# The last two rows of an attention layer get buffers of their own and are normed on VectorE

## The chip, the cores and the metric

The kernel runs on one core of one Trainium2 chip. A core has five engines that run side by side and meet only at semaphores: TensorE (PE; its weight loads are listed as PEld), VectorE (DVE), ScalarE (ACT), GpSimd (POOL) and SyncE (SP), which here only issues DMA transfers. SBUF is the memory on the chip, in 128 partitions; PSUM is the small memory into which TensorE accumulates; DRAM is outside.

The metric is the device time of one execution in microseconds (us), as the median of several runs. Before the change it is 1166.17 us over 3 runs (1164.17 to 1168.2).

## The reference

The program is four layers on a sequence of S = 2048 positions with D = 576 channels, in the order A, B, A, B. Each layer adds its output to its input, and each takes the layer norm of its input first.

```python
x = x + _A_ref(_layernorm(x), A_wqkv, A_wo)
x = x + _B_ref(_layernorm(x), B_w_in, B_w_sp, B_b_sp, B_w_out)
x = x + _A_ref(_layernorm(x), A_wqkv, A_wo)
x = x + _B_ref(_layernorm(x), B_w_in, B_w_sp, B_b_sp, B_w_out)
```

A is attention with 32 heads of 18 channels. A position attends to itself and to seven earlier ones, two apart (a window of 8, dilation 2); the output goes through `wo`.

B is a gated layer with F = 4608:

```python
z = _gelu(einsum('bsd,df->bsf', x, w_in))
z1 = z[..., :Fh]
z2 = _layernorm(z[..., Fh:])
g = einsum('ts,bsf->btf', w_sp, z2) + b_sp[None, :, None]
return einsum('bsf,fd->bsd', z1 * g, w_out)
```

with Fh = F/2 = 2304. The layer norm is `(x - mean) / sqrt(var + 1e-5)`.

## The kernel before

**Rows.** The 2048 positions are 16 row tiles of 128 (NS = 16), one position per partition. In an A layer, row tile `i` holds even positions for `i` below 8 and odd ones above (`rows_of`), since with dilation 2 these do not see each other. The normed input of every layer stands transposed in SBUF, as `xnT` (channels on partitions, positions along it).

**Layer A** lays out Q and K through staging tiles `stg` (PG, with many small transfers), then runs 34 steps (`NST = 2 * NT`): logits (L473), exp on ScalarE (L482), the product with V (PV, L496 to L504). The work of the tail of the layer is hung on those steps in `table`, with `at(step, function, arguments)`; what is hung on a step is issued after PV of that step, in the order in which it was hung, and what is hung past the last step is issued at the end, in order of step. For row tile `i` the pieces are:

- `WO(i, hh)`: five matmuls into `pw` (L557), and an add on VectorE of `pw` and the old x into half of the new x (L560). `x_new` is a ring of four buffers. So the x of row tile `i` takes the buffer of row tile `i - 4`, and waits until that one's norm has read it and its store has landed.
- `XST(i)`: SyncE stores the new x to DRAM (`xres`).
- `LN_STATS`, `LN_AGGR`, `LN_POW`: statistics of the row (L568), mean and variance (L574) and the addition of eps (L581) on VectorE; the power -1/2 on GpSimd (L582).
- `LN_XN(i)`: the norm itself, on GpSimd (`ln_xn`, L259), and a copy of the last 64 channels (L262), into one of four bf16 buffers.
- `XN_ST(i)`: SyncE stores the normed row to a DRAM tensor, `xn_rows`.
- `LN_T(k)`: SyncE reads 128 natural positions of `xn_rows` back with a transposing DMA (L598) into `xnT`. Tiles `2m` and `2m + 1` each need the even and the odd row tile `m` and `m + 8`.

The last four row tiles (12 to 15, `tail_rows`) end too late for the steps. Their statistics, powers and norms all hang on step 37 (`NST + 3`), in two pairs: statistics of 12 and 13, their powers, their norms, and then the same for 14 and 15. The store of the normed row 15 and the transposes of tiles 14 and 15 are put into `deferred`, from which the next layer issues them when it needs those rows. The order on all five engines is the order of the program here (`manual_schedule`).

**Layer B, first part** (p1): the matmuls of z2 (L907) in nine groups of eight units, a unit being 128 positions by 512 channels in a PSUM bank; rows are taken in pairs, nine units to a pair. ScalarE empties the banks through gelu into a row buffer `zp` (L954; three buffers), VectorE takes statistics (L956, L969), GpSimd takes eps and power (L971, L972), and the norm into `Z` (L980) is split: VectorE does eight ninths, GpSimd the last ninth. A `zp` buffer is free again only when both have read it. VectorE and ScalarE work in the order of the program in p1; on SyncE a scheduler chooses the order. In this part it also loads the spatial weights, four `Wq` tiles of 128 x 16 x 512, with transposing DMAs (L877), the bias `b_sp`, and the first z1 weights, which go into a part of `Z` not used so far.

**Layer B, second and third part**: z1 (L1031), the spatial product (L1055) with its gate (L1059, L1060) and the output product (L1104). SBUF of one layer is used again by the next: `Z` of layer B covers the places of `QK` and of the first staging tiles of layer A. A write to such a place waits for those who used it last.

Of the kernel before, what the change touches and what calls it, by code (L numbers as in the profile page):

```python
# [12 lines left out]
f32 = mybir.dt.float32  # L13
# [5 lines left out]
P = 128  # L19
D = 576  # L20
# [43 lines left out]
class K:  # L64
# [274 lines left out]
    def layer_A(self, li):  # L339
        nc, tc, cfg = self.nc, self.tc, self.cfg  # L340
        S, NT, XW, NS = cfg.S, cfg.NT, cfg.XW, cfg.NS
# [12 lines left out]
        stgs = [main.tile([P, 2, CBW], bf16, name=f"stg{k_}") for k_ in range(NSTG if li == 0 else 2)]  # L354
# [11 lines left out]
        sb = sb_cm.__enter__()  # L366
        x_news = [sb.tile([P, D], f32, name="x_new", tag="x_new", bufs=4) for k_ in range(4)]
# [92 lines left out]
        NST = 2 * NT  # L460
# [27 lines left out]
        def PV(s):  # L488
            t, hf = divmod(s, 2)
            nk, nq = tdim(t)  # L490
            O_ps = self.PT_tile([P, 512], f32, "O_ps")
            for jp, js in enumerate(((0, 1, 2), (3,))):
                for ftl in range(4):
                    for jj, j in enumerate(js):
                        idx = 4 * ftl + j
                        nc.tensor.matmul(O_ps[:, idx * (DH + 1):(idx + 1) * (DH + 1)],  # L496
                                         lhsT=P_bufs[2 * jp + s % 2][:nk, jj, ftl, :],
                                         rhs=v_ext[:nk, t, 16 * hf + idx, :], start=True, stop=True)
            Ov = O_ps[:, 0:16 * (DH + 1)].rearrange("p (h e) -> p h e", e=DH + 1)
            o_t = o_bufs[t % len(o_bufs)]  # L500
            rec = sb.tile([P, 16], f32, name="rec", tag="rec", bufs=2)
            nc.vector.reciprocal(out=rec[:], in_=Ov[:, :, DH])
            LN_AGGR()
            nc.vector.tensor_tensor(out=o_t[:, 288 * hf:288 * (hf + 1)].rearrange("p (h d) -> p h d", d=DH),  # L504
                                    in0=Ov[:, :, 0:DH], in1=rec[:, :, None].to_broadcast([P, 16, DH]), op=ALU.mult)
            LN_POW()
            if hf == 1 and t < NT - 2:
                if in_ring(t):
                    c0 = q0_(t) % (RING * P)
                    n0 = min(P, RING * P - c0)  # L510
                    nc.sync.dma_start_transpose(out=oT[:, :, c0:c0 + n0], in_=o_t[0:n0, :])
                    if n0 < P:
                        nc.sync.dma_start_transpose(out=oT[:, :, 0:P - n0], in_=o_t[n0:P, :])
                else:
                    nc.sync.dma_start_transpose(out=o_slots[(t // 2) % NSLOT][:], in_=o_t[:, :])
# [16 lines left out]
                nc.scalar.copy(out=oT[:, :, c0:c0 + n], in_=pt[:, :, a:a + n])  # L532

        tails = {}
        xnd = self.dram.tile([S, 640], bf16, name=f"xn_rows{li}")

        def xo_of(p):
            if li == 0:
                return p % 3
            return p % 2 if p < 4 else (2, 0, 1)[(p - 4) % 3]  # L540
# [9 lines left out]
        def WO(i, hh):  # L550
            st = tails[i]
            if hh == 0:
                st["x"] = x_news[i] if i < 4 else sb.tile([P, D], f32, name="x_new", tag="x_new", bufs=4)
            r0 = (i % RING) * P
            pw = self.PT_tile([P, 512], f32, "pw")
            for c in range(5):
                nc.tensor.matmul(pw[:, 0:288], lhsT=oT[:, c, r0:r0 + P], rhs=wo_sb[:, c, hh * 288:(hh + 1) * 288],  # L557
                                 start=(c == 0), stop=(c == 4))
            hs = slice(hh * 288, (hh + 1) * 288)
            nc.vector.tensor_tensor(out=st["x"][:, hs], in0=pw[:, 0:288], in1=st["xo"][:, hs], op=ALU.add)  # L560
# [9 lines left out]

        def LN_AGGR():
            for i, st in owed:
                mv = sb.tile([P, 2], f32, name="ln_mv", tag="ln_mv", bufs=3)
                nc.vector.bn_aggr(out=mv[:], in_=st[:])  # L574
                tails[i]["ln"] = mv

        def LN_POW():
            for i, _ in owed:
                mv = tails[i]["ln"]
                rstd = sb.tile([P, 1], f32, name="ln_rstd", tag="ln_rstd", bufs=3)  # L580
                nc.vector.tensor_scalar(out=rstd[:], in0=mv[:, 1:2], scalar1=EPS, scalar2=None, op0=ALU.add)  # L581
                nc.gpsimd.tensor_tensor(out=rstd[:], in0=rstd[:], in1=self.neg_half[:], op=ALU.pow)  # L582
                tails[i]["ln"] = mv, rstd, None
            owed.clear()

        def LN_REST():
            LN_AGGR()
            LN_POW()

        def LN_XN(i):  # L590
            mv, rstd, nmr = tails[i].pop("ln")
            tails[i]["xn"] = self.ln_xn(tails[i]["x"], P, mv, rstd, nmr, eng="pool")

        def XN_ST(i):
            self.dma(self.rows_of(xnd, i), tails.pop(i)["xn"])
# [155 lines left out]
        def at(s, f, *a):  # L751
            table.setdefault(s, []).append((f, a))
# [27 lines left out]
        tail_rows = []  # L780
        for i in range(NS):
            s, s1 = wo_steps[i]
            if i % 2 == 0:
                last = [j for j in range(i) if xo_of(j // 2) == xo_of(i // 2)][-1:]
                at(max([s - 7] + [wo_steps[j][1] + 1 for j in last]), XO, i)
            at(s, WO, i, 0)
            at(s1, WO, i, 1)
            if s1 < NST - 1:
                at(s1, LN_STATS, i)
                at(s1 + 1, LN_XN, i)  # L790
            else:
                tail_rows.append(i)
            at(s1 + 1, XST, i)
            if i < NS - 1:
                at(s1 + 4, XN_ST, i)
            if NS // 2 <= i < NS - 1:
                for k_ in range(2):
                    at(max(s1 + 6, NST + 3 * (i - NS // 2) - 4), LN_T, 2 * i - NS + k_)
        for k_ in range(0, len(tail_rows), 2):
            for i in tail_rows[k_:k_ + 2]:  # L800
                at(NST + 3, LN_STATS, i)
            at(NST + 3, LN_REST)
            for i in tail_rows[k_:k_ + 2]:
                at(NST + 3, LN_XN, i)
        at(2 * (NT - 3) + 3, O_CP, NT - 3)
        if li == 0:
            at(0, self.load_wo, nc.sync)
# [28 lines left out]
        for s in sorted(table):  # L836
            for f, a in table[s]:
                f(*a)
        self.deferred.append(((NS - 2) * P, lambda: XN_ST(NS - 1)))
        for k_ in (NS - 2, NS - 1):  # L840
            self.deferred.append((k_ * P, lambda k_=k_: LN_T(k_)))
        man.__exit__(None, None, None)
# [374 lines left out]
```

## Time and profile before

| | |
|---|---|
| median of 3 runs | 1166.17 us (1164.17 to 1168.2) |
| the profiled execution, its span from the first to the last instruction | 1170.2 us |
| mean granted TensorE clock | 0.997 |
| p1 of the first layer B, from its first matmul to the first of z1 | 126.39 to 201.93 us |
| p1 of the second layer B | 702.62 to 775.80 us |
| POOL `ln_xn` L259, one norm of 128 x 576 | 2.29 us, 32 of them |
| ACT `zp` waiting for POOL `Z`, first and second p1 | 9.2 and 10.8 us in all |
| PE `pzs` waiting for ACT `zp`, first and second p1 | 1.0 and 0.5 us |

The profile is of one execution, recorded by the hardware. Of the profiled execution only the span is known; no other time stands beside it. Its views are: a page with the busy time of each engine; the busy time by stretches, with the granted TensorE clock; the chain of work that ended last, followed back from the end; the instructions of an engine in order of time; and the groups of like instructions. In the rows in order of time, the first number is the start in us from the beginning of the span and the second the time that the merged instructions took; a bracket at the end tells how long the engine was idle before the row, and which instruction released it. SPq rows are DMA issues: the time of a row is the issue, not the transfer. In the chain, a DMA row is a transfer from issue to landing.

### The profile page before, as it was taken

How to read it: one execution, taken by the hardware profiler on the slowest of the kernel's cores; microseconds unless marked ns; L12 is line 12 of the kernel's file. 1: busy time of each engine (PE TensorE's matmuls, PEld its weight loads, DVE VectorE, ACT ScalarE, POOL GpSimd, SP SyncE). 2: the span in 40 equal slices, each digit the busy share in tenths (PEclk: the TensorE clock that was granted, in tenths of full speed). 3: DMA queues.
4: the chain of work that ended last, by engine and by line, in shares of the span. 5: the costliest groups of instructions: out<-in, count | busy, mean ns of one | idle time of the engine just before them, and what ended most of it. 6: DMA issues, size and time to landing. Idle time of an engine off the chain costs nothing.

```text
span 1170.2 us, 19968 instructions
## 1 busy us (share of the span) xinstructions
PE 1150.5 (98%) x8163; PEld 612.5 (52%) x8258; DVE 550.0 (47%) x1167; ACT 338.8 (29%) x493; POOL 278.8 (24%) x389
## 2 busy tenths in 40 slices
PE   9999999999999999999999999999999999999998
PEld 5457544444444444457755774444444444444677
DVE  8668598322333332244555886963322223322321
ACT  5589455111100111101247884541011110111000
POOL 4659865000000000001153786640000000000000
PEclk9999999999999999999999999999999999999999
DMA  9599697000000000049646997930000000001332
GB/s 217 119 160 294 193 212 142 23 12 12 12 1 12 12 12 1 6 138 296 169 107 105 204 256 182 242 91 1 12 12 12 12 12 1 12 1 46 111 105 74
DMA packets 183240, 106.45 MB, mean 91 GB/s; under 512 B 135225, under 2 KB 164441, under 8 KB 183149
## 3 DMA queue, kind: packets, MB, share of 16 engines
q1 hardware_dynamic: 170285, 84.85, 31.6%
q0 software_dynamic: 6512, 14.57, 4.8%
q10 hardware_dynamic: 6352, 5.75, 1.6%
q8 instruction: 64, 1.05, 0.4%
q14 instruction: 27, 0.22, 0.1%
HBM read 42.40 MB, written 21.77 MB: 55 GB/s over the span
## 4 chain that ended last, share of the span: by engine, by line
PE 85%; POOL 7%; DMA 3%; DVE 2%; issue 2%; ACT 0%; SPq 0%; POOLq 0%; DVEq 0%; ACTq 0%
PE pg L1055 42%; PE po L1104 12%; PE pz L1031 6%; PE pz1s L1031 6%; PE pzs L907 5%; PE pp L436 4%; PE pz L907 4%; POOL ln_xn L259 4%; PE pv L410 2%; PE O_ps L496 1%; PE pw L557 1%; PE L_ps L473 1%; POOL ln_rstd L582 1%; DMA QK<-stg 1%; DMA o_slot<-o_t 1%
## 5 line engine op out<-in xcount | busy, mean ns | idle before, releaser
L1055 PE MATMUL pg<-Wq,Z 128*128 128x512 bf16 x2260 | 497.9, 379 | 2.5
L1055 PEld LDWEIGHTS <-Z 128*128 128x128 bf16 x2304 | 225.5, 98 | 271.8
L1059 DVE TENSOR_TENSOR g_tmp<-pg,ln_xn 128x512 f32<-128x512 f32 x144 | 99.6, 692 | 421.5 <-PE pg L1055 419.5
L1050 ACT ACTIVATE z1T<-pz 128x1024 bf16<-128x1024 f32 x36 | 34.9, 1021 | 500.8 <-PE pz L1031 500.8
L78 POOL DMA_DIRECT2D wout<-in_B_w_out_dram x4 | 4.3, 1070 | 598.8 <-PE pg L1055 598.8
L1104 PE MATMUL po<-wout,Z 128*128 128x288 bf16 x1152 | 141.4, 286 | 0.0
L482 ACT ACTIVATE P_sb<-L_ps 128x1440 bf16<-128x1440 f32 (+3 forms) x136 | 125.1, 972 | 21.1 <-PE L_ps L473 19.7
L1104 PEld LDWEIGHTS <-Z 128*128 128x128 bf16 x1152 | 112.7, 98 | 28.8
L907 PEld LDWEIGHTS <-xnT 128*128 128x128 bf16 (+1 forms) x800 | 68.7, 98 | 80.0 <-issue 15.5
L1060 DVE TENSOR_TENSOR Z<-g_tmp,z1T 128x512 bf16<-128x512 f32 x144 | 99.7, 692 | 12.2
L956 DVE BATCH_NORM_STATS2 z_st<-zp 128x6 f32<-128x512 bf16 (+1 forms) x160 | 91.0, 617 | 5.1 <-ACT zp L954 4.8
L1031 PEld LDWEIGHTS <-w 128*128 128x128 bf16 (+1 forms) x640 | 53.7, 97 | 74.0 <-issue 13.6
L436 PE MATMUL pp<-xnT,wqk_sb 128*128 128x512 bf16 x341 | 82.2, 382 | 2.5 <-DVE o_t L504 1.3
L259 POOL TENSOR_SCALAR ln_xn<-x_new,ln_mv,ln_rstd 128x576 bf16<-128x576 f32 x32 | 73.3, 2291 | 2.6
L1114 DVE TENSOR_TENSOR x_new<-po,xo 128x288 f32<-128x288 f32 (+1 forms) x64 | 28.8, 455 | 87.4 <-PE po L1104 83.9
L1031 PE MATMUL pz<-xnT,w 128*128 128x512 bf16 (+1 forms) x316 | 66.3, 380 | 0.2
L1031 PE MATMUL pz1s<-xnT,w 128*128 128x512 bf16 (+1 forms) x310 | 64.9, 379 | 0.9 <-issue 0.8
L78 POOL DMA_DIRECT2D QK<-stg x81 | 49.5, 614 | 46.0 <-DVE oT L524 14.8
L907 PE MATMUL pzs<-win2a,xnT 128*128 128x512 bf16 (+1 forms) x235 | 59.9, 364 | 0.4 <-issue 0.3
L907 PE MATMUL pz<-win2a,xnT 128*128 128x512 bf16 (+1 forms) x233 | 58.3, 357 | 0.6 <-issue 0.2
L980 POOL TENSOR_SCALAR Z<-zp,z_mv,z_rstd 128x256 bf16<-128x256 bf16 x32 | 55.7, 1740 | 3.4
L436 PEld LDWEIGHTS <-wqk_sb 128*128 128x128 bf16 x360 | 33.5, 98 | 38.3 <-DVE o_t L504 1.5
(113 smaller groups left out, 936.6 us busy)
## 6 DMA issues: line engine op xcount, KB each, us to landing
xres<-x_new SPq DMA_DIRECT2D x48, 288.0 KB
xo<-xres SPq DMA_DIRECT2D x32, 288.0 KB
wout<-in_B_w_out_dram POOLq DMA_DIRECT2D x4, 1296.0 KB, 8.2
xn_rows<-ln_xn SPq DMA_DIRECT2D x32, 160.0 KB
w<-in_B_w_in_dram SPq DMA_DIRECT2D x16, 256.0 KB
QK<-stg POOLq DMA_DIRECT2D x55, 72.0 KB, 5.2
xo<-xres SPq DMA_DIRECT2D x6, 576.0 KB
QK<-stg SPq DMA_DIRECT2D x39, 72.0 KB
```

Of the source, the lines that this page charges most:

```text
L78: return eng.dma_start(out=out, in_=in_)
L259: e.tensor_scalar(out=xn[:nrows, 0:D], in0=x_t[:nrows, :], scalar1=mv[:nrows, 0:1], scalar2=rstd[:nrows, 0:1], op0=ALU.subtract, op1=ALU.mult)
L436: nc.tensor.matmul(pp[:, :], lhsT=w, rhs=self.xnT[:, c, cc * 512:(cc + 1) * 512], start=(c == 0), stop=(c == 4))
L482: nc.scalar.activation(out=P_bufs[2 * jp + s % 2][:nk, :, :, 0:nq], in_=Lv[:nk, :, :, 0:nq], func=ACT.Exp, scale=scale)
L907: nc.tensor.matmul(out[:, o0:o0 + n], lhsT=self.xnT[r0:r1, c, r * P:(r + 1) * P], rhs=win2(c)[r0:r1, w0:w0 + n], start=start, stop=stop, t ...
L956: nc.vector.bn_stats(out=st[:, x // 512, :], in_=zp[:, x:x + min(512, w0 + n - x)])
L980: eng.tensor_scalar(out=Z[:, b0:b1, i, :], in0=zv[:, b0:b1, :], scalar1=mv[:, 0:1], scalar2=rstd[:, 0:1], op0=ALU.subtract, op1=ALU.mult)
L1031: nc.tensor.matmul(outs[a_], lhsT=w1[r0:r1, c, sub * P:(sub + 1) * P], rhs=self.xnT[r0:r1, c, q * 512:(q + 1) * 512], start=start, stop=st ...
L1055: nc.tensor.matmul(pg[:, :], lhsT=Z[:, jj, i, sub * P:(sub + 1) * P], rhs=Wq[q][:, i, :], start=(i == 0), stop=(i == NS - 1))
L1059: nc.vector.tensor_tensor(out=tmp[:], in0=pg[:, :], in1=bsp[:, qs], op=ALU.add)
L1060: nc.vector.tensor_tensor(out=uT(jj)[:, sub, qs], in0=tmp[:], in1=z1Ts[jj, sub][:, qs], op=ALU.mult)
L1104: nc.tensor.matmul(acc[hh], lhsT=u_rows(j, i), rhs=wouts[j // NJH][:, j % NJH, hh * 288:(hh + 1) * 288], start=(j == 0), stop=(j == NJ - 1))
```

## The change

In layer A of both kinds (first and second):

- `late_rows` cuts the first two staging tiles `stg` into a float32 part of 576 (a row's x) and a bf16 part of 640 (its normed row). `WO` uses them for row tiles 14 and 15 instead of the `x_new` ring, and `LN_XN` writes their normed rows there.
- `LN_XN` of row tiles 14 and 15 goes to VectorE; 12 and 13 stay on GpSimd.
- All statistics and powers of the four tail rows are issued first, and the four norms after them, so that GpSimd's four powers stand ahead of its two remaining norms. `ln_mv` and `ln_rstd` get five buffers each instead of three.
- The stores of the normed rows 14 and 15 are hung on step 37, the last ones of that step, ahead of those of 12 and 13 (step 38). The transposes of tiles 4 and 5 move from step 36 to step 38, behind the stores of 14 and 15. The store of row 15 is no longer deferred.

In the program that comes out, TensorE and ScalarE have the same instructions in the same order as before. On SyncE the order after row 10's normed store is: x of 12 and 13, normed 11, x of 14 and 15, normed 14 and 15, transposes 4 and 5, normed 12 and 13, ten transposes (6 to 15), the first `Wq`, `b_sp`, three `Wq`, and then the first z1 weights (`Z<-in_B_w_in_dram`), which the scheduler had placed before the normed stores of 12 and 13. Transposes 14 and 15, before, stood behind the first `Wq`.

```diff
         tails = {}
+        late_rows = []
+        for k_ in range(2):
+            flat = stgs[k_][:].rearrange("p a b -> p (a b)")
+            late_rows.append((flat[:, 0:2 * D].bitcast(f32), flat[:, 2 * D:2 * D + 640]))
...
             if hh == 0:
-                st["x"] = x_news[i] if i < 4 else sb.tile([P, D], f32, name="x_new", tag="x_new", bufs=4)
+                if i >= NS - 2:
+                    st["x"], st["xn"] = late_rows[i - NS + 2]
+                else:
+                    st["x"] = x_news[i] if i < 4 else sb.tile([P, D], f32, name="x_new", tag="x_new", bufs=4)
...
-                mv = sb.tile([P, 2], f32, name="ln_mv", tag="ln_mv", bufs=3)
+                mv = sb.tile([P, 2], f32, name="ln_mv", tag="ln_mv", bufs=5)
...
-                rstd = sb.tile([P, 1], f32, name="ln_rstd", tag="ln_rstd", bufs=3)
+                rstd = sb.tile([P, 1], f32, name="ln_rstd", tag="ln_rstd", bufs=5)
...
             mv, rstd, nmr = tails[i].pop("ln")
-            tails[i]["xn"] = self.ln_xn(tails[i]["x"], P, mv, rstd, nmr, eng="pool")
+            tails[i]["xn"] = self.ln_xn(tails[i]["x"], P, mv, rstd, nmr, eng="dve" if i >= NS - 2 else "pool",
+                                        xn=tails[i].get("xn"))
...
-            if i < NS - 1:
+            if i < NS - 2:
                 at(s1 + 4, XN_ST, i)
             if NS // 2 <= i < NS - 1:
                 for k_ in range(2):
-                    at(max(s1 + 6, NST + 3 * (i - NS // 2) - 4), LN_T, 2 * i - NS + k_)
+                    at(max(s1 + 6, NST + 3 * (i - NS // 2) - 4, NST + 4 if i > NS // 2 + 1 else 0), LN_T, 2 * i - NS + k_)
         for k_ in range(0, len(tail_rows), 2):
             for i in tail_rows[k_:k_ + 2]:
                 at(NST + 3, LN_STATS, i)
             at(NST + 3, LN_REST)
-            for i in tail_rows[k_:k_ + 2]:
-                at(NST + 3, LN_XN, i)
+        for i in tail_rows:
+            at(NST + 3, LN_XN, i)
+        for i in (NS - 2, NS - 1):
+            at(NST + 3, XN_ST, i)
...
-        self.deferred.append(((NS - 2) * P, lambda: XN_ST(NS - 1)))
```

## The prediction

> **What bounds the kernel now.** I read the page first, then the busy time by stretches, then the chain that ended last, then each engine in order of time around the places where TensorE (PE) stood still.
>
> ```profile
> span 1170.2 us, 19968 instructions
> PE 1150.5 (98%) x8163; PEld 612.5 (52%) x8258; DVE 550.0 (47%) x1167; ACT 338.8 (29%) x493; POOL 278.8 (24%) x389
> ```
>
> PE is busy in 98% of the span. The change touches no matmul, so it can gain only where PE waits or runs below its clock. Layer B's first part (p1) is nine equal groups of eight matmul units per layer, each group beginning with a `pz` matmul. I cut the stretches at these beginnings. The columns are the stretch, its length, busy time (and count) of PE, PEld, DVE, ACT and POOL, then the granted TensorE clock, the DMA share and GB/s:
>
> ```profile
> 134.38:142.38 8.00, 7.95 (x46) 3.84 (x46) 4.25 (x11) 3.37 (x6) 7.81 (x9) 1.00 0.65 201
> 142.38:153.97 11.59, 10.33 (x46) 4.35 (x45) 8.13 (x15) 4.55 (x8) 8.85 (x11) 0.85 0.64 141
> 146.80:147.94 1.14, 0.17 (x2) 0.00 (x0) 1.14 (x3) 0.43 (x2) 0.67 (x1) 1.00 0.68 126
> 147.94:152.57 4.63, 4.40 (x13) 1.47 (x13) 4.56 (x11) 2.94 (x5) 2.81 (x4) 0.65 0.55 118
> 718.40:727.84 9.44, 8.64 (x45) 3.95 (x45) 6.58 (x13) 3.09 (x5) 6.89 (x8) 1.00 0.64 140
> 722.82:723.50 0.68, 0.17 (x2) 0.00 (x0) 0.68 (x2) 0.43 (x2) 0.21 (x1) 1.00 0.93 189
> 723.50:724.81 1.31, 1.08 (x6) 0.30 (x5) 1.28 (x4) 1.31 (x3) 0.52 (x2) 1.00 0.51 111
> ```
>
> An undisturbed group takes 8.00 us. The third group of the first B layer takes 11.59 us and that of the second 9.44 us: 3.59 and 1.44 us lost, 5.03 together. Idle time is 1.14 and 0.68 us of it (1.82). The other 3.21 us is matmuls that ran long just after the idle time, in the first layer at a granted clock of 0.65 over 4.63 us. The chain shows what the idle time waited for:
>
> ```profile
> 129.68 0.82 DVE x_new L560 x2
> 130.50 1.45 DVE ln_st L568 x4
> ...
> 133.41 2.29 POOL ln_xn L259
> ...
> 138.56 1.05 POOL ln_rstd L582 x2
> ...
> 144.74 0.21 POOL z_rstd L971
> ...
> 145.71 1.77 POOL Z L980
> ...
> 147.79 1.09 ACT zp L954 x2
> 148.92 1.30 PE pzs L907 x4
> ```
>
> Four attention norms sit on GpSimd (POOL) ahead of the first norm of B, and only that one frees the `zp` buffer into which ScalarE (ACT) must empty PE's PSUM banks. In order of time:
>
> ```profile
> 140.67 0.89 ACT L954 ACTIVATE zp<-pzs 128x512 bf16<-128x512 f32 x2
> 147.51 1.36 ACT L954 ACTIVATE zp<-pzs 128x256 bf16<-128x256 f32 x3 [5.94 <-POOL Z L980]
> 723.07 1.36 ACT L954 ACTIVATE zp<-pzs 128x256 bf16<-128x256 f32 x3 [5.48 <-POOL Z L980]
> 126.46 0.82 DVE L560 TENSOR_TENSOR x_new<-pw,xo 128x288 f32<-128x288 f32 x2 [2.13 <-POOL ln_xn L259]
> 705.12 0.82 DVE L560 TENSOR_TENSOR x_new<-pw,stg 128x288 f32<-128x288 f32 x2 [3.43 <-DMA xres<-x_new]
> 127.35 2.29 POOL L259 TENSOR_SCALAR ln_xn<-x_new,ln_mv,ln_rstd 128x576 bf16<-128x576 f32 x1
> 132.33 1.08 POOL L582 TENSOR_TENSOR ln_rstd<-ln_rstd,neg_half 128x1 f32<-128x1 f32 x2 [2.38 <-DVE ln_rstd L581]
> 136.04 2.79 DVE L956 BATCH_NORM_STATS2 z_st<-zp 128x6 f32<-128x512 bf16 x5
> 138.86 0.29 DVE L969 BATCH_NORM_AGGREGATE z_mv<-z_st 128x2 f32<-128x30 f32 x1
> 145.64 0.81 DVE L980 TENSOR_SCALAR Z<-zp,z_mv,z_rstd 128x2048 bf16<-128x2048 bf16 x1 [5.61 <-POOL z_rstd L972]
> ```
>
> ACT waited 5.94 us, from 141.57 to 147.51, and cost PE 1.14 us. So ACT may start as late as 147.51 - 1.14 = 146.4 without stopping PE. In the second layer the limit is 723.07 - 0.68 = 722.4.
>
> **The change, part by part** (first layer; the second runs alike).
>
> *Own buffers for rows 14 and 15.* The adds of these rows waited for a norm (2.13 us, row 126.46) or a store (3.43 us, row 705.12) to free a shared buffer. With their own, they run as PE delivers: both are done by about 126.9, when PE has ended its last `pw`, instead of 130.5. DVE then does both pairs' statistics (1.45 us a pair, some 0.4 to 0.6 for means and eps): about 128.9 and 130.9. The buffers lie in staging memory, last used when Q and K were laid out. POOL's and DVE's first Z writes cover that memory and so wait for its four stores (below).
>
> *Powers first, two norms off POOL.* POOL is free at 127.35 + 2.29 + 0.3 = 129.95. Four powers at 0.54 end at 132.3, and norms 12 and 13 (2.29, with their 0.24 copy and gaps 2.57 each) end at 137.5. Before, POOL came to B's work at 144.74: 7.2 us are gained there. B's `z_mv` is ready when DVE gets to it. After its two norms, at about 133.3, it needs 2.79 + 0.29: 136.4. So the first z power ends about 138.4, Z at 138.4 + 1.8 = 140.2, before ACT asks at 141.57. PE's wait goes in the first layer. In the second, the same steps start from an add of row 15 at 702.8 (before 705.94): POOL free at about 713.0 and Z at about 715.7, against a limit of 722.4.
>
> *Two norms on DVE.* No row shows this operation on DVE. Below it stands the bf16 form, above it the case in which each norm stands still until the POOL norm beside it ends:
>
> ```profile
> L654 DVE TENSOR_SCALAR ln_xn<-x_in,lnx_mv,lnx_rstd 128x576 bf16<-128x576 bf16 x4 | 1.4, 424 | 3.9 <-POOL lnx_rstd L647 3.9
> 197.50 1.23 POOL L980 TENSOR_SCALAR Z<-zp,z_mv,z_rstd 128x256 bf16<-128x256 bf16 x1
> 130.69 0.87 SPq L78 DMA_DIRECT2D xres<-x_new  x2
> 132.13 2.55 SPq L598 DMA_TRANSPOSE xnT<-xn_rows  x2
> 144.44 7.80 SPq L598 DMA_TRANSPOSE xnT<-xn_rows  x6
> 163.29 1.18 SPq L78 DMA_DIRECT2D ln_xn<-in_B_b_sp_dram  x1
> 164.58 26.96 SPq L877 DMA_TRANSPOSE Wq<-in_B_w_sp_dram  x3
> 699.60 2.53 SPq L598 DMA_TRANSPOSE xnT<-xn_rows  x2
> 702.39 1.62 PEld L907 LDWEIGHTS <-xnT 128*128 128x128 bf16 x9 [0.28 <-DMA xnT<-xn_rows]
> 144.10 0.81 PE L907 MATMUL pz<-win2a,xnT 128*128 128x512 bf16 x3
> 201.93 4.16 PE L1031 MATMUL pz<-xnT,Z 128*128 128x512 bf16 x19
> 702.85 2.15 DMA xres<-x_new
> 66.01 7.66 DMA o_slot<-o_t
> ```
>
> At 0.42 each, plus a small copy, both norms end by 133.3; I take this end, since it is the same operation, shape and engine. At the other end the second waits out both POOL norms, until 137.6. The row at 197.50 speaks for some of that: POOL's Z takes 1.23 us alone and 1.77 beside DVE's Z. Then DVE's first z statistics end at 140.7, Z at about 144.2 and ACT starts near 144.4, still before 146.4: the gain on PE is the same. [...]
>
> *SP's queue.* Stores of rows 14 and 15 now stand ahead of the transposes of rows 4 and 5, which left at 132.13. SP issues six stores, at 0.44 each (row 130.69) or a little more, from 130.0 on, and then waits for the DVE norms: the two transposes leave at about 134.3 (138.0 at the bad end). A transpose lands about 2.9 us after its start (699.60 to the PEld row at 702.39). Row 4 is first needed by the third unit of the third group, at 144.10, so the margin is 6.9 us or 3.2. Staging stores land 2.15 us after issue (row 702.85), by 136.5 or 140.3, before the Z writes at 138.4 or 142. Zero cost, covered by these margins. Next, rows 12 and 13 are stored after POOL's 137.5, and ten transposes at 1.30 end near 151.1, followed by the four Wq at 8.99 and the b_sp load at 1.18: 188.2.
>
> *One unplanned move.* In the changed program, the first z1 weights (written into Z) are issued behind those four Wq; before, they left SP at about 137. They would leave at 188.2 to 189.8 and land 2.15 to 7.66 us later (a quiet and a loaded transfer above): 192 to 197.5. PE wants them at 201.93 - 3.59 = 198.3. Zero cost, with 0.8 us or more to spare; at the bad end of the norms, 3.6 us later, up to 2.8 us over. I take the quiet end, since nothing else follows on this queue.
>
> **Sum.** 3.59 + 1.44 = 5.03 us. The profiled execution, 1170.2 us long, should come to 1165.2. It is 4.0 us above the median of the runs, 1166.17, and above the highest of them, 1168.2; the same subtraction gives **1161.1 us** for the median.
>
> **Rivals.**
> *Only the idle time comes back.* The clock part, 3.21 of 5.03 us, differs between two like stalls: about 2.45 against 0.76. It may be smaller in executions that are not profiled, which are shorter anyhow; that is what speaks for it. Against it: both stalls show some. Gain 1.82, time 1164.35. [...]
>
> *The wait moves.* If the stores of rows 14 and 15 hold SP, rows 4 and 5 reach PE late, and PE waits at 144.10 instead of 146.80. This needs those transposes to start after 141.2, 6.9 us beyond my estimate. If it costs what the old wait cost, nothing changes: 1166.2. Or POOL's first Z waits for the staging stores past 146.4, with the same outcome.
>
> *Slower: the z1 weights.* Behind four Wq they could land after 198.3, and PE would stop at the start of the second part. The price is their lateness, plus clock loss as above, in both layers. To lose 3.5 us in all, they must eat 5.03 and 3.5 more: 4.3 us a layer, landing at 202.6. The worst rows, together, reach 201.1, 2.8 us late: 1164 to 1167 for one layer or both.
>
> **How the numbers follow.** 0.3% (3.5 us) is about what a measurement of this kernel can tell from no change, so faster means below 1162.7. Chances: both losses gone, 0.62 (own range 1159 to 1163); only idle back or little more, 0.22 (1163 to 1165.5); wait moved, 0.09; z1 weights late, 0.07, half of it beyond the rows. Most of the first and a little of the second is faster: 0.63. Same: 0.28. Slower: 0.09, with something unseen counted in. The range is 1158.5 to 1166.5: below, 2.6 us for the spread of the runs (4 us from lowest to highest); above, it reaches past the second case and takes in the moved wait at 1166.2.
>
> **What would show it.** Right: no POOL wait of ACT's `zp` near 141; third groups of 8.00 us; granted clock 1.00 there; POOL's first `z_rstd` near 137.5; stores from staging memory; PE's L1031 matmuls 3.6 and 5.0 us earlier. Wrong: PE or PEld waiting for `xnT` near 144, PE waiting for a DMA of `Z` at the second part's start, or third groups still above 8.00. DVE norms above 0.9 us would show the bad end.

## The result, and the profile after

The changed kernel takes 1164.12 us in the median of 20 runs (1162.09 to 1166.22). The kernel before, run beside it, takes 1167.51 us in the median of 20 (1162.6 to 1173.26). The ratio is 0.9969, with a 95% interval of 0.9957 to 0.998: a gain of 3.4 us by the medians, 2.3 to 5.0 by the interval. Forecast were 1161.1 us and a gain of 5.0.

The page of the changed kernel begins so:

```profile
span 1163.6 us, 19961 instructions
PE 1145.7 (98%) x8163; PEld 610.6 (52%) x8258; DVE 555.0 (48%) x1175; ACT 339.0 (29%) x493; POOL 267.6 (23%) x381
```

POOL works 11.2 us less than before and DVE 5.0 us more. PE's share is still 98%, so it is the stretches that tell. The third group of the first p1 and of the second, in the same columns as in the prediction:

```profile
140.32:148.31 7.99, 7.94 (x45) 3.83 (x45) 7.04 (x14) 4.12 (x7) 4.68 (x6) 1.00 0.58 121
713.20:721.19 7.99, 7.94 (x45) 3.85 (x45) 7.79 (x15) 4.12 (x7) 5.49 (x7) 1.00 0.63 125
```

The third groups that took 11.59 and 9.44 us are now as long as an undisturbed group, at a granted clock of 1.00. POOL and DVE in order of time, at the end of the first attention layer:

```profile
127.83 2.25 POOL L589 TENSOR_TENSOR ln_rstd<-ln_rstd,neg_half 128x1 f32<-128x1 f32 x4
129.93 2.29 POOL L259 TENSOR_SCALAR ln_xn<-x_new,ln_mv,ln_rstd 128x576 bf16<-128x576 f32 x1
132.49 2.29 POOL L259 TENSOR_SCALAR ln_xn<-x_new,ln_mv,ln_rstd 128x576 bf16<-128x576 f32 x1
...
136.05 1.76 POOL L989 TENSOR_SCALAR Z<-zp,z_mv,z_rstd 128x256 bf16<-128x256 bf16 x1
```

```profile
129.46 0.58 DVE L259 TENSOR_SCALAR stg<-stg,ln_mv,ln_rstd 128x576 bf16<-128x576 f32 x1 [0.64 <-POOL ln_rstd L589]
130.07 0.71 DVE L262 COPY stg<-stg 128x64 bf16<-128x64 bf16 x1
130.69 0.57 DVE L259 TENSOR_SCALAR stg<-stg,ln_mv,ln_rstd 128x576 bf16<-128x576 f32 x1
131.30 0.18 DVE L262 COPY stg<-stg 128x64 bf16<-128x64 bf16 x1
```

POOL does four powers, two norms and then B's Z, which ends at 137.81, that is 2.51 us before the third group begins. Before, it ended at 147.48, 5.10 us after the group's begin.

Where the two profiled executions differ, cut at p1's first matmul and at the first of z1:

| stretch | before | after | difference |
|---|---|---|---|
| start to first p1 | 126.39 | 124.33 | -2.06 |
| first p1 | 75.54 | 71.94 | -3.60 |
| between | 500.69 | 501.15 | +0.46 |
| second p1 | 73.18 | 71.73 | -1.45 |
| second p1 to the end | 394.4 | 394.4 | 0.0 |

The two first parts give 5.05 us, the forecast 5.03. So in this pair the sum came out within 0.02 us, and yet the runs gain 3.4. The experiments had to find the missing 1.6 us. The first and third rows cannot be put down to the change: in four profiles of the kernel before, p1 began at 122.57 to 128.54 us, and in two of the changed kernel at 124.33 and 123.85.

### The profile page after: what moved, and what is told of

The parts are those of the page before. It is cut to its first block, busy times and chain, and to the rows that moved or that the text cites. A ratio compares the mean times of both kernels' runs of the same rounds, so it can differ in the third digit from the quotient of the medians.

```text
span 1163.6 us, 19961 instructions
## 1 busy us (share of the span) xinstructions
PE 1145.7 (98%) x8163; PEld 610.6 (52%) x8258; DVE 555.0 (48%) x1175; ACT 339.0 (29%) x493; POOL 267.6 (23%) x381
## 4 chain that ended last, share of the span: by engine, by line
PE 92%; DMA 3%; DVE 2%; issue 1%; POOL 1%; SPq 1%; ACT 0%; DVEq 0%; ACTq 0%; POOLq 0%
PE pg L1064 43%; PE po L1113 12%; PE pz L916 6%; PE pz L1040 6%; PE pz1s L1040 6%; PE pzs L916 6%; PE pp L436 4%; PE pw L564 3%; PE pv L410 2%; PE O_ps L496 2%; PE L_ps L473 1%; DMA o_slot<-o_t 1%; DMA QK<-stg 1%; POOL QK L78 1%; SPq L78 1%
## 5 line engine op out<-in xcount | busy, mean ns | idle before, releaser
L965 DVE BATCH_NORM_STATS2 z_st<-zp 128x6 f32<-128x512 bf16 (+1 forms) x160 | 91.4, 617 | 13.7 <-ACT zp L963 13.5
L259 POOL TENSOR_SCALAR ln_xn<-x_new,ln_mv,ln_rstd 128x576 bf16<-128x576 f32 x28 | 64.1, 2288 | 2.6
L963 ACT ACTIVATE zp<-pz 128x1024 bf16<-128x1024 f32 (+2 forms) x56 | 36.6, 720 | 64.6 <-PE pz L916 64.6
```

The lines of the kernel that those rows point to most:

```text
L259: e.tensor_scalar(out=xn[:nrows, 0:D], in0=x_t[:nrows, :], scalar1=mv[:nrows, 0:1], scalar2=rstd[:nrows, 0:1], op0=ALU.subtract, op1=ALU.mult)
L965: nc.vector.bn_stats(out=st[:, x // 512, :], in_=zp[:, x:x + min(512, w0 + n - x)])
```

## The experiments

### The same kernels again

The kernel before three more times, the changed kernel once more, without edits.

> The kernel before once more, against itself: ratio 1.000, and a second profiled execution. Theory A (the stall's idle time is fixed, the slow matmuls after it differ from execution to execution): the third groups of B's first part are again stopped by ScalarE's wait for GpSimd's Z, with 1.1 and 0.7 us of idle time, but the time above 8.00 us need not be 3.59 and 1.44; anything from 1.8 to 6 us for the two together. Theory B (the stall costs 5.0 us in every execution, and the changed kernel gives 1.5 us back elsewhere): 3.6 and 1.4 us again, within 0.3 us.

> The changed kernel once more. Ratio 0.996 to 0.998 (2.3 to 5 us less than before). Both theories: third groups of 8.00 us and no wait of ScalarE for GpSimd's Z. Theory B: a place outside B's first part that is about 1.5 us longer than in the same run's kernel before, and is longer in both profiles of the changed kernel; the 0.46 us between the two first parts in the first pair is the only candidate so far. Theory A: no such place, the stretches outside the first part agree within 0.5 us.

> The kernel before, a third profiled execution. So far the third group of the first layer lost 3.59 and 0.27 us, that of the second 1.44 and 1.37. Theory A (the first layer's loss depends on how far GpSimd's queue is behind TensorE when the first part begins: its norm of row 11 ended 3.2 us after the start where 3.59 us were lost, 0.9 us after it where 0.27 were): the loss is 0.3 us when that norm ends about 1 us after the start, and 1.9 to 3.6 us when it ends about 3 us after it. Second layer 1.4 us. Theory B (5.0 us in every execution) has already fallen.

> The kernel before, a fourth profiled execution, with the same two cases for the first layer and 1.4 us in the second. A clock below 1.00 behind the stall is expected only where TensorE stood still for more than about 1 us: none after 0.4 to 0.7 us so far, some after 1.1 to 2.9 us.

Measured: before against itself 1.000 (0.9984 to 1.0015); the changed kernel 1164.5 us beside 1166.89, ratio 0.9965 (0.9949 to 0.9981). The third and fourth execution of before took 1172.44 and 1165.32 us. Third groups of the changed kernel's second profile, and then of the three of before (first and second layer each):

```profile
139.84:147.83 7.99, 7.99 (x46) 3.85 (x45) 7.05 (x14) 4.12 (x7) 4.78 (x6) 1.00 0.56 115
712.40:720.40 8.00, 8.00 (x47) 3.85 (x46) 7.79 (x16) 4.13 (x7) 5.53 (x7) 1.00 0.59 124
```

```profile
141.17:149.44 8.27, 8.17 (x46) 3.85 (x45) 6.58 (x13) 3.09 (x5) 5.80 (x8) 1.00 0.59 130
713.49:722.86 9.37, 8.70 (x47) 3.95 (x46) 6.58 (x13) 3.10 (x5) 6.81 (x8) 1.00 0.58 132
```

```profile
144.53:154.44 9.91, 8.65 (x45) 3.93 (x45) 6.58 (x13) 3.09 (x5) 7.43 (x8) 1.00 0.63 137
718.79:728.27 9.48, 8.65 (x46) 3.95 (x46) 6.59 (x13) 3.10 (x5) 6.92 (x8) 1.00 0.63 138
148.95:150.10 1.15, 0.17 (x3) 0.00 (x0) 1.15 (x3) 0.44 (x2) 0.68 (x1) 1.00 0.62 141
150.10:151.40 1.30, 1.07 (x5) 0.30 (x5) 1.27 (x4) 1.30 (x3) 0.51 (x2) 1.00 0.65 122
```

```profile
138.56:146.80 8.24, 8.12 (x46) 3.84 (x46) 6.58 (x13) 3.16 (x5) 5.70 (x8) 1.00 0.61 138
711.81:721.11 9.30, 8.64 (x45) 3.95 (x45) 6.58 (x13) 3.16 (x5) 6.68 (x8) 1.00 0.62 141
```

The loss in the two groups is 5.03 us in the shown profile of before, and 0.27 + 1.37 = 1.64, 1.91 + 1.48 = 3.39 and 0.24 + 1.30 = 1.54 in the others; the changed kernel loses nothing in either of its profiles. Theory A holds: the price of the stall is not a constant. Theory B fell, also because the stretch between the two p1 took 500.69, 500.09, 500.61 and 501.27 us in before, and 501.15 and 500.61 after: it gives nothing back.

Two things make the price differ. The first is how late POOL is when p1 begins. POOL's norm of row 11 (one row from each of two profiles of before, the second and the third):

```profile
123.81 2.29 POOL L259 TENSOR_SCALAR ln_xn<-x_new,ln_mv,ln_rstd 128x576 bf16<-128x576 f32 x1
```

```profile
129.50 2.29 POOL L259 TENSOR_SCALAR ln_xn<-x_new,ln_mv,ln_rstd 128x576 bf16<-128x576 f32 x1
```

It ends 0.92 us after p1's first matmul (125.18) where the first layer lost 0.27, and 3.25 us after it (128.54) where it lost 1.91, as in the shown profile (129.64 - 126.39 = 3.25). In the fourth profile it ends at 1.60, with 0.24 lost. That answers to the expectation, on four executions. Below 1.60 us the loss no longer follows the norm: in the second profile it is a store that row 15's add waits for (at 126.83, 2.22 us for the store of an `x_new`).

The second is the clock. The shown profile and the third have the same stop (PE idle for 1.14 and 1.15 us), and the same wait of ACT of 5.94 us; but the matmuls behind it ran at these granted clocks in the shown profile (the last row is from its first attention layer, and is used further below):

```profile
147.94:149.25 1.31, 1.08 (x6) 0.30 (x5) 1.28 (x4) 1.31 (x3) 0.52 (x2) 1.00 0.67 138
149.35:152.76 3.41, 3.41 (x9) 1.21 (x9) 3.38 (x8) 1.72 (x3) 2.30 (x4) 0.50 0.52 115
...
40.12:43.53 3.41, 3.19 (x12) 1.62 (x11) 0.46 (x1) 0.49 (x2) 3.41 (x6) 0.50 0.77 176
```

and at 1.00 throughout in the third. The difference is 3.59 - 1.91 = 1.68 us, which is about half of 3.41. So my guess of about 1 us as the length from which a stop costs the clock does not hold: with 1.15 us it did not, with 1.14 it did.

These rows also show a mistake in how I had read the profile. In the 1.31 us after the stop the clock is 1.00, and five matmuls still take 1.37 us instead of 0.60. That is no clock loss. The same five matmuls in the changed kernel, and then in the changed kernel with three extra norms on POOL (below), with other engines, in order of time, show what it is:

```profile
144.75 0.60 PE L916 MATMUL pzs<-win2b,xnT 64*128 64x512 bf16 x5
```

```profile
143.47 1.36 ACT L968 ACTIVATE zp<-pzs 128x256 bf16<-128x256 f32 x3 [5.22 <-POOL Z L994]
143.91 1.37 PE L921 MATMUL pzs<-win2b,xnT 64*128 64x512 bf16 x5 [0.26 <-ACT zp L968]
143.91 0.09 PEld L921 LDWEIGHTS <-xnT 64*128 64x128 bf16 x1 [0.54 <-issue]
...
144.40 0.09 PEld L921 LDWEIGHTS <-xnT 64*128 64x128 bf16 x1 [0.40 <-issue]
```

ACT empties bank after bank, 1.36 us for three, and PE can use each only when it is empty: its weight loads come 0.49 us apart, as ACT's evictions do (in the shown profile of before these end at 147.89, 148.38 and 148.87 us, and the loads start at 147.94, 148.43 and 148.92). The stop goes on as a slow walk of 1.37 - 0.60 = 0.77 us that the profile counts as busy.

### One part alone

Only the buffers of rows 14 and 15 (edit of the kernel before; the normed rows stay in the shared buffers, the norms on POOL, the order as before):

```diff
-                st["x"] = x_news[i] if i < 4 else sb.tile([P, D], f32, name="x_new", tag="x_new", bufs=4)
+                if i >= NS - 2:
+                    st["x"] = late_rows[i - NS + 2][0]
+                else:
+                    st["x"] = x_news[i] if i < 4 else sb.tile([P, D], f32, name="x_new", tag="x_new", bufs=4)
```

> Only rows 14 and 15's sums go to their own buffers; order of powers and all four norms on GpSimd as before. In the time of the shown profile of before: sums done at 126.9, GpSimd free at 130.0, two powers 131.0, two norms 136.2, two powers 137.2, two norms 142.4, Z near 144.9, which is 1.5 us before ScalarE's being late stops TensorE (146.4). If the limit is right: no idle time of TensorE in either layer and the same gain as the whole change, ratio 0.996 to 0.998. Rival (each of the three parts is needed): idle time of 0.5 us or more in a third group, and a third to two thirds of the gain.

Only VectorE's norms, the order of powers and the order of stores and transposes (edit of the changed kernel; the sums of rows 14 and 15 are back in the shared buffers):

```diff
                 if i >= NS - 2:
-                    st["x"], st["xn"] = late_rows[i - NS + 2]
-                else:
-                    st["x"] = x_news[i] if i < 4 else sb.tile([P, D], f32, name="x_new", tag="x_new", bufs=4)
+                    st["xn"] = late_rows[i - NS + 2][1]
+                st["x"] = x_news[i] if i < 4 else sb.tile([P, D], f32, name="x_new", tag="x_new", bufs=4)
```

> Rows 14 and 15's sums stay in the shared buffers, their norms go to VectorE and the powers of all four rows go first. The sums are held back as before (done at 130.5 in the time of the shown profile of before), the four powers end near 135.4, GpSimd's two norms near 140.5, Z near 142.9, 3.5 us before the limit of 146.4: no idle time and the same gain as the whole change, ratio 0.996 to 0.998. Rival (the sums' buffers are what matters): ScalarE's wait for Z stays and the ratio is 0.999 or more.

Measured: 1164.23 us, ratio 0.9965 (0.9949 to 0.9981), and 1165.11 us, ratio 0.9975 (0.9958 to 0.9991). Both third groups of the first kernel, then of the second, and POOL's first Z of each in order of time:

```profile
141.94:149.94 8.00, 8.00 (x47) 3.85 (x46) 7.09 (x14) 3.72 (x6) 5.44 (x8) 1.00 0.59 130
714.05:722.05 8.00, 8.00 (x47) 3.85 (x45) 7.80 (x15) 4.66 (x8) 5.54 (x7) 1.00 0.61 135
```

```profile
142.85 1.76 POOL L987 TENSOR_SCALAR Z<-zp,z_mv,z_rstd 128x256 bf16<-128x256 bf16 x1
```

```profile
139.04:147.04 8.00, 8.00 (x47) 3.85 (x46) 7.80 (x16) 4.66 (x8) 5.52 (x7) 1.00 0.65 149
715.21:723.20 7.99, 7.99 (x46) 3.85 (x45) 7.75 (x16) 4.45 (x8) 5.16 (x6) 1.00 0.61 126
```

```profile
138.06 1.76 POOL L988 TENSOR_SCALAR Z<-zp,z_mv,z_rstd 128x256 bf16<-128x256 bf16 x1
```

Either part alone removes both stops. Z ends 2.67 us (142.85 + 1.76 - 141.94) and 0.78 us after the third group's begin. Neither could be told by its time from the whole change, which had 0.9965 beside the same runs of before. The parts do not add up: each brings Z's end inside the limit worked out below, and what lies beyond buys only distance from it. The buffers alone leave the least of it.

### How late POOL may be

The changed kernel with N norms more on POOL, behind row 13's (N = 2, 3 and 4; the output goes to a tile that is written anew before it is read):

```diff
             tails[i]["xn"] = self.ln_xn(tails[i]["x"], P, mv, rstd, nmr, eng="dve" if i >= NS - 2 else "pool",
                                         xn=tails[i].get("xn"))
+            if i == NS - 3:
+                for _ in range(N):
+                    nc.gpsimd.tensor_scalar(out=P_bufs[0][:].rearrange("p a b c -> p (a b c)")[:, 0:D],
+                                            in0=tails[i]["x"][:, :], scalar1=mv[:, 0:1], scalar2=rstd[:, 0:1],
+                                            op0=ALU.subtract, op1=ALU.mult)
```

> The changed kernel with two more GpSimd norms of 128x576 (2.29 us each and a gap of 0.05, results thrown away) behind row 13's norm, in both layers. In the changed kernel GpSimd's first Z ends 13.5 us after the first part's start, and would end at 13.5 + 2 x 2.34 = 18.2. ScalarE may be as late as 19.1 or 19.2 without stopping TensorE (the second profile of before: start at 19.48, 0.27 us lost; its second layer: 20.59, 1.37 lost). So nothing is lost: third groups of 8.00 us, ratio as without the two, 0.996 to 0.998. Rival (GpSimd's work counts at once, or the limit lies earlier): third groups of 9 us and more, ratio 0.999 or more.

> The changed kernel with three more GpSimd norms behind row 13's. Z ends 20.5 us after the start in the first layer and 20.2 in the second, where the bound is 19.1 to 19.2: 1.3 and 1.1 us lost, third groups of 9.3 and 9.1 us, of which TensorE stands still for only 0.5 and 0.3 us and paces itself by ScalarE's three evictions for the rest. With the clock at 1.00 after so short a stop: 2.4 us against the changed kernel, ratio 0.998 to 0.999. With a clock loss behind each stop as after the longer ones: up to 3.4 us more, ratio 1.001 to 1.002.

> The same with four more norms. Z ends 13.5 + 9.4 = 22.9 us after the start in the first layer and about 22.5 in the second. Waits alone: lost 22.9 - 19.2 = 3.7 and 22.5 - 19.1 = 3.4, 7.1 us against the changed kernel, ratio 1.002 to 1.003 against before. With a clock loss behind each stall, such as the 1.7 us in the first layer of the shown profile of before (granted clock 0.65): 10.5 us, ratio 1.005 to 1.006.

Measured, for N = 2, 3 and 4: 1165.39, 1165.48 and 1175.37 us; ratios 0.9971 (0.9954 to 0.9987), 0.999 (0.9976 to 1.0005) and 1.006 (1.0033 to 1.0087). Third groups, first and second layer, for N = 2, 3 and 4, and for N = 4 the matmuls behind the second layer's stop:

```profile
139.51:147.51 8.00, 7.95 (x45) 3.85 (x45) 7.74 (x15) 4.49 (x8) 5.41 (x8) 1.00 0.61 124
711.55:719.54 7.99, 7.94 (x45) 3.85 (x45) 7.58 (x15) 4.34 (x8) 5.41 (x8) 1.00 0.61 125
```

```profile
139.06:148.25 9.19, 8.65 (x46) 3.95 (x45) 6.58 (x13) 3.16 (x5) 6.71 (x7) 1.00 0.58 124
712.32:721.55 9.23, 8.65 (x45) 3.94 (x45) 6.58 (x13) 3.16 (x5) 6.67 (x7) 1.00 0.61 127
```

```profile
140.33:153.19 12.86, 10.02 (x45) 4.20 (x45) 7.58 (x15) 4.24 (x8) 10.09 (x11) 0.87 0.56 117
719.25:732.43 13.18, 10.32 (x45) 4.39 (x45) 8.13 (x15) 4.56 (x8) 10.34 (x11) 0.87 0.65 138
...
727.71:731.46 3.75, 3.75 (x13) 1.53 (x12) 3.71 (x8) 2.07 (x4) 2.65 (x4) 0.54 0.57 120
```

Set against the end of POOL's first Z, counted from the third group's begin, all profiles without a clock loss lie on one line:

| kernel, layer | Z ended after | lost | difference |
|---|---|---|---|
| N = 2, both | 1.89, 2.04 | 0 | |
| only buffers, first | 2.67 | 0 | |
| before, fourth and second profile, first layer | 3.43, 3.46 | 0.24, 0.27 | 3.19, 3.19 |
| N = 3, both | 4.38, 4.42 | 1.19, 1.23 | 3.19, 3.19 |
| before, second layer, four profiles | 4.49, 4.56, 4.64, 4.67 | 1.30, 1.37, 1.44, 1.48 | 3.19, 3.19, 3.20, 3.19 |
| before, third profile, first layer | 5.10 | 1.91 | 3.19 |
| before, shown profile, first layer | 5.10 | 3.59 | (1.68 us of clock above the line) |
| N = 4, both | 6.91, 6.68 | 4.86, 5.18 | (1.14 and 1.69 us of clock above the line) |

By this line POOL is free to be late up to 3.19 us after the group's begin, and from there on every microsecond is one lost. The groups with a clock loss lie above the line by what the clock took. N = 3 puts the stall of before back: 2.42 us in the profile, and its ratio of 0.999 is 0.0021 above the 0.9969 of the changed kernel, which is 2.5 us. By the runs alone the step from N = 2 to N = 3 would not be shown: the intervals overlap, and the two ran beside different sets of before (medians 1168.62 and 1167.13), so that their own medians, 1165.39 and 1165.48, cannot be set against each other. The profiles show it. N = 4 came out with the clock loss, as its second value had it (10.04 us lost in the profile, 1.006 in the runs).

### The order alone

First try (edit of the changed kernel: buffers and norms as before, but the new order of the powers and the new order of stores and transposes):

```diff
-                if i >= NS - 2:
-                    st["x"], st["xn"] = late_rows[i - NS + 2]
-                else:
-                    st["x"] = x_news[i] if i < 4 else sb.tile([P, D], f32, name="x_new", tag="x_new", bufs=4)
+                st["x"] = x_news[i] if i < 4 else sb.tile([P, D], f32, name="x_new", tag="x_new", bufs=4)
...
-            tails[i]["xn"] = self.ln_xn(tails[i]["x"], P, mv, rstd, nmr, eng="dve" if i >= NS - 2 else "pool",
+            tails[i]["xn"] = self.ln_xn(tails[i]["x"], P, mv, rstd, nmr, eng="pool",
                                         xn=tails[i].get("xn"))
```

> Only the order is changed: the powers of all four rows ahead of the four norms, which stay on GpSimd, with the shared buffers as before. The sums are held back as before; the four powers end 8.9 us after the first part's start (as with the norms on VectorE and shared buffers), four norms of 2.57 at 19.2, Z at 22.0 against 21.1 in the shown profile of before: the first layer loses 2.9 us by waits where before loses 1.9, the second about 2.2 against 1.4. Ratio 1.001 to 1.003. Rival (the order helps by itself): ratio below 0.999 and shorter third groups than before.

Measured: 1192.15 us, ratio 1.0206 (1.0178 to 1.0233): a miss of 20 us. Third groups, SP's queue, and PE in order of time:

```profile
140.78:161.32 20.54, 9.96 (x45) 4.29 (x45) 11.34 (x21) 4.89 (x9) 11.05 (x14) 0.75 0.83 189
726.57:748.00 21.43, 10.27 (x46) 4.36 (x46) 11.33 (x21) 4.89 (x9) 10.81 (x13) 0.68 0.85 187
```

```profile
140.95 0.35 SPq L78 DMA_DIRECT2D xn_rows<-ln_xn  x1
141.35 8.10 SPq L883 DMA_TRANSPOSE Wq<-in_B_w_sp_dram  x1
149.56 0.50 SPq L78 DMA_DIRECT2D xn_rows<-ln_xn  x1
150.11 2.53 SPq L603 DMA_TRANSPOSE xnT<-xn_rows  x2
```

```profile
153.03 1.46 PE L913 MATMUL pz<-win2a,xnT 128*128 128x512 bf16 x3 [10.36 <-DMA xnT<-xn_rows]
```

I had followed POOL's queue and not SP's. The new order of stores puts rows 14 and 15 ahead of the transposes of tiles 4 and 5. With VectorE's norms these stores leave early; with POOL's they wait for its last norm, the scheduler sets an 8.1 us `Wq` between them, and tile 4 reaches PE 10.4 us late. This run does not test the order of powers, but it shows that the new order of stores rests on VectorE's norms: with them, and the same shared buffers, that order lost nothing in the profile of the run above (1165.11 us).

Second try (edit of the kernel before, five buffers for `ln_mv` and `ln_rstd` beside it):

```diff
-            for i in tail_rows[k_:k_ + 2]:
-                at(NST + 3, LN_XN, i)
+        for i in tail_rows:
+            at(NST + 3, LN_XN, i)
```

> The kernel before with one edit: the powers of the last four rows ahead of their four norms, all on GpSimd. The stores and transposes on SyncE stay in the order of before, unlike in the run in which the stores of rows 14 and 15 held the transposes of rows 4 and 5 up. Z then ends 21.4 us after the start in the first layer and 21.0 in the second (as GpSimd's rows show in that run), against 19.45 to 21.1 and 20.4 to 20.6 in before: 2.2 and 1.9 us lost by waits, 4.1 in all, where before loses 1.6 to 3.4; with clock losses 1.7 us a layer more. Ratio 1.001 to 1.004. Rival (the order alone brings a part of the gain): below 0.999.

Measured: 1169.37 us beside 1167.13, ratio 1.002 (1.0 to 1.004), as expected; the third groups:

```profile
141.80:153.82 12.02, 10.05 (x45) 4.25 (x45) 7.73 (x15) 4.44 (x8) 9.13 (x13) 0.86 0.61 137
718.38:730.22 11.84, 10.29 (x46) 4.34 (x46) 8.09 (x15) 4.56 (x8) 9.03 (x11) 0.86 0.63 134
```

Z ended 5.93 and 5.38 us after the begins: 2.74 and 2.19 us by the line, the rest clock. The order of the powers alone makes it no better, if anything worse, since POOL waits for the second pair's statistics before it norms the first pair.

### All four norms on VectorE

```diff
-            tails[i]["xn"] = self.ln_xn(tails[i]["x"], P, mv, rstd, nmr, eng="dve" if i >= NS - 2 else "pool",
+            tails[i]["xn"] = self.ln_xn(tails[i]["x"], P, mv, rstd, nmr, eng="dve" if i in tail_rows else "pool",
```

> The changed kernel with all four last norms on VectorE, so that GpSimd is idle beside them. Z ends about 14 us after the first part's start, no gain and no loss against the changed kernel: ratio 0.996 to 0.998. [...]

Measured: 1167.14 us (1161.75 to 1172.58), ratio 0.999 (0.9968 to 1.0012). Its third group in the first layer, and VectorE's first two norms in order of time:

```profile
137.59:145.58 7.99, 7.94 (x45) 3.84 (x45) 6.80 (x14) 4.12 (x7) 4.53 (x6) 1.00 0.59 124
```

```profile
126.01 0.58 DVE L259 TENSOR_SCALAR ln_xn<-x_new,ln_mv,ln_rstd 128x576 bf16<-128x576 f32 x1
126.62 0.18 DVE L262 COPY ln_xn<-ln_xn 128x64 bf16<-128x64 bf16 x1
126.71 0.57 DVE L259 TENSOR_SCALAR ln_xn<-x_new,ln_mv,ln_rstd 128x576 bf16<-128x576 f32 x1
```

In the profile nothing is lost, as expected, and the second norm takes the same 0.57 us with no norm on POOL beside it as the changed kernel's second, which lay wholly inside one of POOL's: POOL's norms did not hold it up. The first small copy took 0.71 us beside POOL's norm and takes 0.18 here. The runs miss the expectation of 0.996 to 0.998. Why the median is no better than before is not settled: the one profiled execution, 1161.89 us, is among the fastest of its 12, and the granted clock of the others reaches down to 0.996 without a profile that tells where.

## Why the prediction was right, and where it was wrong

**The two losses go: right.** Third groups of 8.00 us in both layers and both profiles, no wait of ACT for POOL's Z, clock 1.00, first parts shorter by 3.60 and 1.45 us.

**The steps on POOL and DVE: right within half a microsecond.** Counted from p1's start, POOL was forecast to come to B's work at 11.1 us and did at 10.7 (135.04); Z to end at 13.8, and it did at 13.5. The DVE norms were to end at 6.9 (good end) and ended at 7.15. A norm costs 0.58, not 0.42. The good end was right: the second norm ran wholly inside POOL's norm of 129.93 to 132.22 (the first had all but ended when it began) and was not held.

**The limit: too late by 0.8 us.** I put it at 146.4, 4.0 us after the third group's begin, by the first bank that PE needs. It lies at 3.19, because PE also needs the second and third bank, which ACT empties one after the other, 0.49 us apart. (A small misreading beside it: from 699.60 to 702.39 are 2.79 us for a transpose to land, not 2.9, which leaves SP a margin of 7.0 us.) Nothing came of the limit here, since Z ended 5.7 us ahead; for the buffers alone (2.67) the margin is 0.52 us and not 1.35.

**The split of the loss: wrong.** I had 1.82 us idle and 3.21 us at a slower clock. By the rows it is 1.82 us idle, 1.53 us at the pace of ACT's evictions (0.77 and 0.76), and 1.68 us of clock. Waits were 3.35 us of 5.03. And behind the second layer's stop the clock stood at 1.00 (the row 723.50 to 724.81 in the prediction), so "both stalls show some" does not hold for the clock part: the first alone does.

**From the profile to the median: the step that failed.** "The same subtraction gives 1161.1 us for the median" took the stall of one execution as that of all. It was the heaviest of four: 5.03, 1.64, 3.39 and 1.54 us, 2.9 on average. The medians give 3.4 and, in the second comparison, 2.4. The forecast missed by 3.0 us: 1.6 from this term, and 1.3 because the 3 runs of before that I started from had a median of 1166.17 and 20 runs have 1167.51. The 4.0 us by which I put the shown execution above the median set a span against times of runs: in the later runs the time lies 1.7 to 1.8 us above the span (1165.39 us for 1163.6 in the changed kernel), so by this estimate it stood some 5.8 us above the median.

**The time itself: in the wrong case.** With both losses gone I expected 1159 to 1163 us, and "faster" below 1162.7. The losses went, and the time is 1164.12, above both and inside the 1163 to 1165.5 that I gave to the rival. That it still lies within 1158.5 to 1166.5 says little, since that range was made to hold the rival and the moved wait as well; what bears the mechanism out is the profiles.

**The rival "only the idle time comes back"** gave 1164.35, and 1164.12 came out; but not for its reason. More than the idle time comes back, since the evictions' pace is part of the wait. Its premise was right: the clock part is a matter of the execution, one of eight lost stretches in four profiles of before.

**The wait moves, the z1 weights: neither.** SP did what was forecast: transposes 4 and 5 left 7.8 us after p1's start (7.9 forecast). The first-try run shows the moved wait with its mechanism, but with a price of 12.5 us or more a layer instead of the old wait's. The z1 weights left SP from 184.31 to 186.60, which is 60.0 to 62.3 us after p1's start, near the 61.8 of the forecast; PE came to them at 196.27 without a wait for a transfer.

**Staging stores at "zero cost": right in price, wrong in margin.** I let them land before the Z writes. In the second layer they did not, all engines in order of time:

```profile
709.70 0.81 DVE L989 TENSOR_SCALAR Z<-zp,z_mv,z_rstd 128x2048 bf16<-128x2048 bf16 x1 [1.58 <-DMA xn_rows<-stg]
709.77 1.77 POOL L989 TENSOR_SCALAR Z<-zp,z_mv,z_rstd 128x256 bf16<-128x256 bf16 x1 [0.98 <-DMA xn_rows<-stg]
```

This new wait costs nothing, as Z still ends 1.66 us before the group begins, 4.85 us ahead of the limit.

## What to carry to other kernels

A stall seen in one profile is one draw: before its length goes into a forecast, look at it in several executions, and split it into the wait, the pace of whoever releases the buffers, and the clock, since the first two lay on one line in all the profiles here, and the third came and went with the execution. When several edits attack one wait, work out for each how far beyond the limit it goes; here the buffers alone were enough, and the rest was margin. And when a store moves ahead of a load on a queue, ask who produces what it stores: the same order that cost nothing with one engine cost 26 us in the profile with another.

## What the runs showed of the hardware

The clock after a stop. Of the stops in the third groups, none with about 0.7 us of idle PE or less was followed by a lower clock (before in its second layer four times, N = 3 twice). With 1.14 us one was and with 1.15 us one was not; with more (1.44 us and up: N = 4 and the two runs of the order alone, in both layers) all were. The slow stretch of the shown profile is 3.41 us at 0.50 (149.35 to 152.76); in N = 4, the 3.75 us behind the second layer's stop stand at 0.54 (727.71 to 731.46). What decided between 1.14 and 1.15 us is not shown.

Such stretches are not tied to this stall. The shown profile has one more in its first attention layer (3.41 us at 0.50, 40.12 to 43.53, shown above). The third profile of before, the fourth, and the one with only the buffers stand at 1.00 in both third groups, and at 0.997, 0.999 and 0.999 in the mean of the execution, so they lost clock elsewhere; the second profile of before and the two of the changed kernel have 1.000. By an estimate from the 3.41 us at 0.50, such a stretch costs PE at most half of that, 1.7 us (1.68 us behind the shown stop), and so is a part of what sets two executions of one kernel apart.

VectorE beside POOL's norms. Inside POOL's norm (from 129.93 to 132.22 in the changed kernel), the first small bf16 copy on VectorE took 0.71 us and the second 0.18; with no norm on POOL, in the run with all four norms on VectorE, the first takes 0.18 as well. The second float32 norm took 0.57 us inside POOL's norm and 0.57 without one. The first copy took 0.53 us longer and ended at 130.78, 1.4 us before POOL's norm did, and neither the second copy nor the norm between them was held, so VectorE did not wait for the end of POOL's norm. What held the first copy stays open.
